# Fifteen transfers of a few bytes queued between the last pieces of an attention block's output weights

## The chip, the cores and the metric

The kernel runs on one core of a Trainium2 chip. It is one launch with bfloat16 inputs and a bfloat16 output. The metric is device microseconds (us) for one execution, and lower is better. A core has four compute engines that run side by side: TensorE (PE in the profile; its weight loads are listed as PEld), VectorE (DVE), ScalarE (ACT) and GpSimd (POOL). A fifth, SyncE (SP), issues data transfers. Sixteen DMA engines carry these transfers out. A transfer is issued by an engine's sequencer, waits in that issuer's queue, runs, and announces its end by counting up a semaphore.

## The reference: what is computed

One token `x` (1024 numbers) goes through two blocks, and a gate mixes their outputs. Cut to what matters:

```
q = x @ wq                            # 32 heads of 128
p = softmax(q . k_cache / sqrt(128))  # 4 key/value heads, 65536 positions, 8 query heads on each
a = (p . v_cache) @ wo                # wo: 4096 x 1024
z = gelu(x @ w_in);  z1, z2 = halves of z, z2 layer-normed
b = (z1 * (w_sp * z2 + b_sp)) @ w_out
g = sigmoid(sum(x * gate_w))
out = g * a + (1 - g) * b             # 1024 numbers
```

The caches are 64 MB each in bfloat16 and every byte of them is used once; `wo` and `wq` are 8 MB each. Reading them is most of what the kernel does: the trace counts 162.01 MB read.

## The kernel before, in words

**Memory.** One SBUF tensor, `arena`, holds everything. The list of regions after L190 gives each region its offset in order, so a region appended at the end moves none of the others. Its first region, `RING`, is five slots of 32 KB per partition that the large inputs pass through.

**The stream of loads.** `load` (L307) appends each large load to the list `stream`: `wq`, the keys, the two weights of the second block, then keys and values in turn, and last `wo`. `wo` is split in four quarters of 1024 rows. The first three are one transfer each. The last quarter is cut by `WO_CUT` into three pieces of 5/8, 2/8 and 1/8 (1280, 512 and 256 KB). I call them piece A, piece B and piece C. Each lies across all 128 partitions; a partition's share is one contiguous run of 10,240, 4,096 or 2,048 bytes.

**The order of the transfers.** `issue` (L376 to L391) walks the stream. It puts one `dma_start` (L389) on SP's queue for each entry, as soon as everything that used the target's place has been recorded as used, and stops at the first entry whose place is still needed. Instructions of one engine run in the order in which they are recorded, so SP issues the stream in its order, each entry after its wait. Just before the last entry, piece C, `issue` calls `store()` (L366) once: an early transfer of the still empty output row. The real store is recorded at the end of the program. Both are transfers of 8 rows of 256 bytes from `orow` to `out`.

**Waits.** The `Recorder` (L18) derives the waits. An operation that reads a key waits for the key's last writer; a DMA gets a semaphore of its own name (`dma=`), and a reader waits for that semaphore's full count of 16 (L108). Waits on other engines are at L110.

**The end of the program.** After the last values, `wo_rows` multiplies the first two quarters of `wo` with the attention output, `wo_piece(2)` the third quarter, and `wo_piece(3, c0, c1)` the three pieces of the last: 40, 16 and 8 matmuls at L712 into one accumulator `fbt`, each piece after its own load. `spin` runs a few matmuls whose result is not used. DVE then copies `fbt` to `orow` (L775), and SP stores it (L366). POOL has nothing to do after its copies at L490, the last of which ends near 245 us.

Of the kernel before, what the change touches and what calls it, by code (L numbers as in the profile page):

```python
# [138 lines left out]
def bass_gated_mix__gqa_block_cached__mixer_gmlp__decode_kernel(  # L139
# [23 lines left out]
    FC = FH // 128  # L163
# [12 lines left out]
    QW = DO // NW  # L176
# [11 lines left out]
    def region(name, nbf):  # L188
        nonlocal cur
        OFF[name] = cur  # L190
        cur += (nbf + 15) // 16 * 16

    for name, n in [
        ("RING", NSUB * SUB), ("KT", NKT * 4096), ("SC", NSC * 2048), ("PSB", 2 * 1024), ("PTSB", 2 * 1024),
        ("QPAD", 4 * QP), ("IDB", 128), ("BM", 256), ("SEL", 16 * 32),
        ("M16", 32), ("MQ", 32), ("XT", KC), ("WB", 2), ("WBB", 4), ("ONEB", 128),
        ("MAXC", 2 * total), ("LP", 2 * total), ("COLS", 2 * 64), ("DM", 64), ("ONES", 256), ("QALL", 128), ("OVZ", 32 * OC + 31), ("E4Z", 128), ("MHALF", 4),
        ("YB", FC), ("OROW", QW),
    ]:
        region(name, n)  # L200
    NA = (cur + 63) // 64 * 64
# [2 lines left out]
    def ab(name, n, o=0):  # L204
        return arena[:, OFF[name] + o:OFF[name] + o + n]
# [4 lines left out]
    def vw(base, off, dims, p0=0, np_=128):  # L210
        ps = base.ap[0][0]
        return bass.AP(tensor=base.tensor, offset=base.offset + off + p0 * ps,
                       ap=[[ps, np_]] + [list(d) for d in dims])
# [41 lines left out]
    P = R.op  # L255
# [46 lines left out]
    stream = []  # L302
# [42 lines left out]
    for i in range(6):  # L345
        a = 2 * i + 4
# [18 lines left out]
    def store():  # L365
        P("SP", lambda e: e.dma_start(out[0, 0].rearrange("(q n) -> q n", n=QW), osrc), r=["orow"],  # L366
          w=["out"], dma="out")

    issued = [0]
    used = set()  # L370
    owner = {}

    def grains(off, w):
        return list(range(off // GRAN, (off + w + GRAN - 1) // GRAN))

    def issue():  # L376

        while issued[0] < len(stream):
            n = issued[0]
            keys, off, src = stream[n]  # L380
            w = src.shape[1]
            gr = grains(off, w)
            if any(k not in used for x in gr if x in owner for k in owner[x]):
                return
            for j, x in enumerate(gr):
                owner[x] = (keys[j * len(keys) // len(gr)],)
            if n == len(stream) - 1:
                store()
            P("SP", lambda e, o=OFF["RING"] + off, w=w, src=src: e.dma_start(arena[:, o:o + w], src),  # L389
              w=[("slot", x) for x in gr], dma="s%d" % gr[0])  # L390
            issued[0] += 1  # L391

    def use(key):
        n, off, w = place[key]
        assert n < issued[0], key
        return arena[:, OFF["RING"] + off:OFF["RING"] + off + w], [("slot", x) for x in grains(off, w)]

    def done(key):
        used.add(key)
        issue()  # L400

    issue()


# [8 lines left out]
      r=["m32"], w=["sel"])  # L413
    P("DVE", lambda e: e.tensor_reduce(mq, vw(idf, 0, [[1, 16], [16, 8]]), AXX, ALU.add), r=["idf"], w=["mq"])
    P("DVE", lambda e: e.tensor_reduce(mhalf, vw(idf, 0, [[32, 2], [64, 2], [1, 32]]), mybir.AxisListType.XY, ALU.add),
      r=["idf"], w=["mhalf"])
# [4 lines left out]
    for fe in range(4):  # L421
        P("POOL", lambda e, fe=fe: e.tensor_copy(vw(sele, 128 * fe, [[32, 4], [1, 32]]),
                                                vw(idb, 64 * (fe // 2) + fe % 2, [[0, 4], [2, 32]])),
          r=["idb"], w=[KSE])
# [5 lines left out]
    def f(e):  # L430
        for c in range(KC):
            ins = e.matmul(tb[:, c:c + 1], vw(xm, c, [[8, 128]], 0, 8), oneb[0:8, 0:1], start=(c == 0),  # L432
                           stop=(c == KC - 1), skip_group_check=True)
        return ins
# [3 lines left out]
      r=["oneb", "wsp", "bsp"], w=["mb"])  # L438
# [6 lines left out]
      r=["ones", "gs"], w=[KTB])  # L445
# [4 lines left out]
      r=["g"], w=["omg"])  # L450
# [254 lines left out]
    def wo_piece(i, c0=0, c1=8):  # L705
        sl, keys = use(("wo", i, c0))
        def f(e, i=i, sl=sl, c0=c0, c1=c1):
            for c in range(c0, c1):
                for s, b, j in SLOTS:
                    o = DO * (c - c0) + QW * s  # L710
                    z = 31 + 32 * (8 * i + c) - j
                    ins = e.matmul(fb[32 * b:32 * (b + 1), 0:QW], ovz[:, z:z + 32],  # L712
                                   sl[:, o:o + QW], start=False, stop=(i == 3 and c == 7),
                                   tile_position=(0, 32 * b), skip_group_check=True)
            return ins
        P("PE", f, r=[("ovec", i)] + keys, w=["fb"])
        done(("wo", i, c0))
# [54 lines left out]
    spin(3)  # L772
    for c0, c1 in WO_CUT:
        wo_piece(3, c0, c1)
    P("DVE", lambda e: e.tensor_copy(orow[0:W0 + NW, :], fb[0:W0 + NW, 0:QW]), w=["orow", "fb"])  # L775
    store()

# [31 lines left out]
```

## Time and profile before

| | us |
|---|---|
| median of 3 runs | 381.85 (381.62 to 381.86) |
| span of the profiled execution, first to last instruction | 380.3 |
| what lies around the span (median less span) | 1.55 |
| PE busy | 235.1 |
| DVE busy | 204.6 |
| ACT busy, POOL busy | 23.3, 8.4 |
| DMA: mean rate over the span | 426 GB/s |

The profile is one execution of the program. Busy time says how long an engine worked; a wait is put down to what ended last before it. "Landing" is the moment at which a transfer's semaphore is full. Besides the views of the page, the trace keeps a record of each DMA packet (its queue, size, start and duration), and the moments at which each of the 16 parts of a transfer counted up its semaphore. A packet is one contiguous run of one partition, or the 4 bytes that close a transfer on one DMA engine. The records do not name the DMA engine.

### The profile page before, as it was taken

The numbers are of one execution on the slowest core, as the hardware profiler recorded it, in microseconds if no ns is written. First come the engines' busy times: TensorE is split into PE (matmuls) and PEld (weight loads), VectorE is DVE, ScalarE is ACT, GpSimd is POOL, SyncE is SP. The second block draws the span as 40 slices with busy tenths as digits, with TensorE's granted clock in tenths as the row PEclk, the third lists the DMA queues.
The fourth block names the chain that finished last, engine by engine and source line by source line (L and its number), as shares of the span: only waits on it lengthen the run. The fifth ranks groups of instructions, "written<-read, shape, count | busy, mean of one in ns | idle before, by whom it ended". The sixth has DMA issues, their size and how long they took to land.

```text
span 380.3 us, 2581 instructions
## 1 busy us (share of the span) xinstructions
PE 235.1 (62%) x1449; PEld 58.1 (15%) x836; DVE 204.6 (54%) x162; ACT 23.3 (6%) x24; POOL 8.4 (2%) x37
## 2 busy tenths in 40 slices
PE   0061388458558924895788138952895884739378
PEld 0010011011111200122112001220121110212015
DVE  4011496778389525965892249745774882312020
ACT  1000000010420000002200000022000000220000
POOL 5000000000000000000000000000000000000000
PEclk9998599696859985998699859995899697958689
DMA  9999999999999999999999999999999999999996
GB/s 435 427 420 400 469 388 438 441 469 431 401 414 441 441 443 427 434 410 424 477 441 434 434 434 414 415 441 441 434 407 433 445 441 441 436 403 424 419 426 262
DMA packets 4254, 162.17 MB, mean 426 GB/s; under 512 B 532, under 2 KB 532, under 8 KB 788
## 3 DMA queue, kind: packets, MB, share of 16 engines
q1 hardware_dynamic: 4208, 162.01, 98.9%
q8 instruction: 9, 0.15, 0.2%
q10 hardware_dynamic: 36, 0.00, 0.0%
q14 instruction: 1, 0.01, 0.0%
HBM read 162.01 MB, written 0.00 MB: 426 GB/s over the span
## 4 chain that ended last, share of the span: by engine, by line
DMA 56%; PE 23%; DVE 18%; ACT 1%; issue 1%; SPq 0%; ACTq 0%; DVEq 0%
DMA arena<-in_A_k_cache_dram 34%; DVE arena L502 15%; DMA arena<-in_A_wo_dram 10%; DMA arena<-in_A_v_cache_dram 8%; PE scp L260 7%; PE scp L262 6%; DMA arena<-in_B_b_sp_dram 5%; PE obt L260 4%; PE obt L262 4%; DVE arena L539 1%; PE fbt L712 1%; PE fbt L660 1%; ACT arena L534 1%; SPq L389 0%; ACTq L288 0%
## 5 line engine op out<-in xcount | busy, mean ns | idle before, releaser
L502 DVE STREAM_TRANSPOSE arena<-arena 128x2048 f32<-128x2048 f32 x64 | 143.0, 2284 | 48.2 <-DMA arena<-in_A_k_cache_dram 32.7
L260 PE MATMUL scp<-arena 128*128 128x512 bf16 (+1 forms) x275 | 112.8, 429 | 87.7 <-DVE arena L502 86.3
L262 PE MATMUL scp<-arena 128*128 128x512 bf16 (+1 forms) x279 | 113.1, 427 | 0.0
L260 PE MATMUL obt<-arena 128*64 128x512 bf16 (+2 forms) x334 | 62.9, 419 | 17.5 <-DMA arena<-in_A_v_cache_dram 17.5
L262 PE MATMUL obt<-arena 128*64 128x512 bf16 (+2 forms) x334 | 62.2, 414 | 0.0
L260 PEld LDWEIGHTS scp<-arena 128*128 128x128 bf16 (+1 forms) x275 | 27.7, 104 | 200.1 <-issue 101.3
L539 DVE STREAM_TRANSPOSE arena<-arena 128x2048 bf16<-128x2048 bf16 x7 | 16.2, 2311 | 28.5 <-PE obt L262 26.4
L534 ACT ACTIVATE arena<-arena 128x2048 bf16<-128x2048 f32 x8 | 16.0, 2002 | 218.6 <-DVE arena L531 195.6
L260 PEld LDWEIGHTS obt<-arena 128*64 128x64 bf16 (+1 forms) x334 | 18.3, 113 | 70.7 <-issue 56.1
L519 DVE TENSOR_SCALAR_CACHE_REDUCE arena<-scp 128x2048 f32<-128x2048 f32 x8 | 18.3, 2292 | 16.0 <-PE scp L262 16.0
L580 PE MATMUL mbt<-arena 128*128 128x128 bf16 x16 | 1.9, 258 | 12.6 <-DVE arena L575 12.6
L542 DVE STREAM_TRANSPOSE arena<-arena 128x1024 bf16<-128x1024 bf16 x2 | 2.5, 1246 | 12.7 <-PE obt L262 12.7
L490 POOL COPY arena<-arena 32x32 bf16<-32x32 bf16 x16 | 3.2, 203 | 234.5 <-PE scp L262 209.7
L568 DVE RECIPROCAL arena<-mbt 128x1 f32<-128x1 f32 x4 | 0.6, 139 | 14.1 <-PE mbt L563 14.1
L531 DVE TENSOR_REDUCE arena<-mbt 128x1 f32<-128x32 f32 x4 | 0.8, 192 | 13.5 <-PE mbt L528 13.5
L437 PE MATMUL mbt<-arena 1*128 1x2 bf16 x1 | 0.2, 158 | 12.3 <-DMA arena<-in_B_b_sp_dram 12.3
L439 DVE COPY arena<-mbt 128x2 f32<-128x2 f32 x1 | 0.2, 160 | 12.3 <-PE mbt L437 12.3
L775 DVE CAST arena<-fbt 36x128 bf16<-36x128 f32 x1 | 0.3, 283 | 11.0 <-PE fbt L712 11.0
L432 PE MATMUL scp<-arena 8*128 8x1 bf16 x8 | 0.7, 199 | 8.7 <-DVE arena L427 8.7
L712 PE MATMUL fbt<-arena 128*32 128x128 bf16 x128 | 4.1, 220 | 0.1
L712 PEld LDWEIGHTS fbt<-arena 128*32 128x32 bf16 x128 | 3.6, 97 | 1.6 <-DMA arena<-in_A_wo_dram 0.8
L467 DVE CAST arena<-obt 97x1024 bf16<-97x1024 f32 x1 | 1.2, 1225 | 4.9 <-PE obt L262 4.9
(91 smaller groups left out, 54.2 us busy)
## 6 DMA issues: line engine op xcount, KB each, us to landing
arena<-in_A_k_cache_dram SPq DMA_DIRECT2D x6, 4096.0 KB, 33.1
arena<-in_A_v_cache_dram SPq DMA_DIRECT2D x2, 4096.0 KB, 26.0
arena<-in_B_w_in_dram SPq DMA_DIRECT2D x1, 7168.0 KB, 30.4
arena<-in_A_wo_dram SPq DMA_DIRECT2D x3, 2048.0 KB, 33.4
arena<-in_B_w_out_dram SPq DMA_DIRECT2D x1, 3584.0 KB, 21.5
arena<-in_A_wo_dram SPq DMA_DIRECT2D x1, 1280.0 KB, 30.3
arena<-in_A_wo_dram SPq DMA_DIRECT2D x1, 512.0 KB, 31.0
arena<-in_A_wo_dram SPq DMA_DIRECT2D x1, 256.0 KB, 30.8
```

The source lines that it names most:

```text
L260: return e.matmul(*a, **kw)
L262: one = e.matmul(*a, **kw).ins
L467: P("DVE", lambda e: e.tensor_copy(psb[0:97, :], ob[0:97, :]), w=["psb", "ob"])
L490: P("POOL", lambda e, pb=pb: e.tensor_copy(vw(qpad, 24 + 32 * pb, [[QP, 4], [1, 8]], 32 * pb, 32), vw(qall, 8 * g, [[32, 4], [1, 8]], 32 * ...
L502: P("DVE", lambda e: e.transpose(ktb(i).bitcast(F32), sl[:, 4096 * p:4096 * (p + 1)].bitcast(F32)), r=keys[4 * p:4 * p + 4], w=[("kt", i % ...
L519: P("DVE", lambda e: e.tensor_scalar(scs(j), scp[:, :], 0.0, None, op0=ALU.add, op1=ALU.max, accum_out=maxc[:, j:j + 1]), w=[("sc", j % 2) ...
L534: P("ACT", lambda e: e.activation(psb2, scs(j), ACTF.Exp, bias=gcol(j // 2, K_NB), scale=SCALE, accum_out=lp[:, j:j + 1]), r=[("sc", j % 2 ...
L539: P("DVE", lambda e: e.transpose(ptsb2, psb2), r=["psb"], w=[("ptsb", 0), ("ptsb", 1)])
L542: P("DVE", lambda e: e.transpose(ptsb(n), ab("PSB", 1024, 1024 * (n % 2))), r=["psb"], w=[("ptsb", n % 2)])
L580: ins = e.matmul(mb[:, 0:128], sel[:, 128 * c:128 * (c + 1)], osc[:, 128 * c:128 * (c + 1)], start=(c == 0), stop=(c == 3))
L660: ins = e.matmul(fb[32 * b:32 * (b + 1), 0:QW], e4z[0:97, 31 - j:63 - j], part[0:97, QW * s:QW * (s + 1)], start=(first and s % (NW // 2) ...
L712: ins = e.matmul(fb[32 * b:32 * (b + 1), 0:QW], ovz[:, z:z + 32], sl[:, o:o + QW], start=False, stop=(i == 3 and c == 7), tile_position=(0 ...
```

## The change

A strip `PRB` of 32 elements (64 bytes) per partition is added at the end of the list of regions. A function `prefixes` queues fifteen transfers on SP. The transfer number k reads two bfloat16 numbers (4 bytes) from each of the first k rows of `A_wq` and puts them into the first k partitions of the strip, at a place of their own. They are issued after piece A of the last quarter of `wo` and before piece B. Each has a semaphore of its own. One POOL copy of one element, recorded after the last matmuls, waits for all fifteen. Nothing reads that element.

```diff
-        ("YB", FC), ("OROW", QW),
+        ("YB", FC), ("OROW", QW), ("PRB", 32),
...
+    prb = ab("PRB", 32)
+
+    def prefixes():
+        for k in range(1, 16):
+            def f(e, k=k):
+                with nc.allow_non_contiguous_dma(reason="a few bytes"):
+                    return e.dma_start(prb[0:k, 2 * k:2 * k + 2], A_wq[0:k, 2 * k:2 * k + 2])
+            P("SP", f, w=[("prb", k)], dma="p%d" % k)
...
             P("SP", lambda e, o=OFF["RING"] + off, w=w, src=src: e.dma_start(arena[:, o:o + w], src),
               w=[("slot", x) for x in gr], dma="s%d" % gr[0])
             issued[0] += 1
+            if n == len(stream) - 3:
+                prefixes()
...
     for c0, c1 in WO_CUT:
         wo_piece(3, c0, c1)
+    P("POOL", lambda e: e.tensor_copy(prb[0:1, 0:1], prb[0:1, 2:3]), r=[("prb", k) for k in range(1, 16)], w=["prb0"])
     P("DVE", lambda e: e.tensor_copy(orow[0:W0 + NW, :], fb[0:W0 + NW, 0:QW]), w=["orow", "fb"])
     store()
```

## The prediction, as it was put on record before the change was run

> **What bounds the kernel.** I read the page first: the busy shares, then the DMA rows, then the chain of waits at the very end, then SP's own timeline. PE is busy 62% of the span and DVE 54%, but the DMA engines are full from the first slice to the last but one:
>
> ```profile
> DMA  9999999999999999999999999999999999999996
> ...
> q1 hardware_dynamic: 4208, 162.01, 98.9%
> q8 instruction: 9, 0.15, 0.2%
> q10 hardware_dynamic: 36, 0.00, 0.0%
> ```
>
> The row of digits is the share of the 16 DMA engines in use; q1 is SP's queue and fills 98.9% of them. So the transfers of SP are the bound, and whatever is put into them ahead of the last one is on the path, unless the DMA engine that carries it has time to spare. The chain of waits, cut to its last microseconds, shows who waits for that last one:
>
> ```profile
> 376.41 0.08 issue
> 376.50 1.77 PE fbt L712 x56
> 378.27 0.01 issue
> 378.27 0.42 PE fbt L712 x8
> ...
> 378.79 0.28 DVE arena L775
> ```
>
> and the timeline of the same stretch, with the idle time and its releaser in brackets:
>
> ```profile
> 378.27 0.23 PEld L712 LDWEIGHTS fbt<-arena 128*32 128x32 bf16 x8 [0.18 <-DMA arena<-in_A_wo_dram]
> 378.79 0.28 DVE L775 CAST arena<-fbt 36x128 bf16<-36x128 f32 x1 [11.04 <-PE fbt L712]
> 379.10 0.31 SPq L366 DMA_DIRECT2D out_dram<-arena  x1
> ```
>
> The 56 matmuls of pieces A and B are issued by 378.27, and the 8 of piece C start there. PE's weight loads had been idle for 0.18 us, waiting for piece C. A delay of piece C is therefore passed on in full to PE, DVE and the store. An earlier piece C could gain at most about that 0.18 us.
>
> **How far SP is ahead of the DMA engines.** SP's timeline (start, duration), then the DMA issues of the page (KB, us to landing):
>
> ```profile
> 345.71 1.28 SPq L389 DMA_DIRECT2D arena<-in_A_wo_dram  x3
> 347.03 0.37 SPq L366 DMA_DIRECT2D out_dram<-arena  x1
> 347.44 0.35 SPq L389 DMA_DIRECT2D arena<-in_A_wo_dram  x1
> ```
>
> ```profile
> arena<-in_A_wo_dram SPq DMA_DIRECT2D x1, 1280.0 KB, 30.3
> arena<-in_A_wo_dram SPq DMA_DIRECT2D x1, 512.0 KB, 31.0
> arena<-in_A_wo_dram SPq DMA_DIRECT2D x1, 256.0 KB, 30.8
> ```
>
> The three issues from 345.71 are the third quarter, A and B: 1.28 / 3 = 0.43 us each. C follows at 347.44. A starts about 346.1 and lands 30.3 later, at 376.4; B at 346.55 + 31.0 = 377.6; C at 347.44 + 30.8 = 378.2. The DMA engines reach B some 28 us after it was issued, because that much work lies in the queue before it.
>
> **The change, part by part.**
>
> *Fifteen issues on SP.* They stand before B, the early store and C. The nearest rows are the issues of few rows:
>
> ```profile
> L288 ACTq DMA_DIRECT2D arena<-in_A_x_dram x1: 562/562/562, 0.1 to 0.1; - x1
> L288 ACTq DMA_DIRECT2D arena<-in_B_w_sp_dram x1: 273/273/273, 1.0 to 1.0; - x1
> L366 SPq DMA_DIRECT2D out_dram<-arena x2: 309/338/367, 347.0 to 379.1; - x2
> ```
>
> With 0.04 us between issues, fifteen take between 15 x 0.31 = 4.7 and 15 x 0.60 = 9.0 us; I take 15 x 0.41 = 6.2, by the early store's 0.37 + 0.04. C is then issued at 353.6 (at most 356.4) in place of 347.44. The first DMA engine finishes A at about 375, so 18 us of cover are left. SP's next work, the real store, waits for DVE until 379.10. Cost: nothing. Without the cover it would be the whole 6.2 us.
>
> *Packets in the DMA queues.* The page's q10 row tells how a small transfer is cut. ACT issues two transfers of 8 rows and two of one element, and q10 has 36 packets: 2 x (8 + 8) + 2 x (1 + 1). So a transfer of k rows uses k DMA engines, with one data packet and one closing packet on each. The fifteen add 1 + 2 + ... + 15 = 120 data and 120 closing packets. If the first k engines are taken each time, the first engine gets 15 pairs, the eighth 8, the ninth 7, the fifteenth 1, the sixteenth none. "DMA: Bandwidth & Descriptors" of the Trainium skill, section "Why a DMA increments its semaphore by 16 and not by 1", states just this choice of the lowest-numbered k; the trace does not name engines.
>
> What does a pair cost? In the packet records one engine's packets follow each other end to start. On q10 a 2-byte packet starts at 13.849 and the engine's next one at 13.854; closing packets of 4 bytes hold their engine 6 ns as well, and a 256-byte row of the early store 14 ns. A pair is about 12 ns, 28 at the most if a 4-byte row is as dear as a 256-byte row and its closing packet too.
>
> Now which engine is last. C's 16 closing counts come at 376.57 to 376.65 (five), 376.96, 377.06, and 377.89 to 378.23 (nine). Of the nine late chains of packets, three carry a row of the early store, so they belong to the first eight engines; their closing packets start at 377.43, 377.50 and 377.54. The other six have none, so they are among the second eight; theirs start from 377.58 to 377.815, and the last of these ends the load (378.23).
> - A late engine of the first eight has 0.27 us to spare against 377.815. Fifteen pairs of 12 ns are 0.18 us: hidden. At 28 ns they are 0.42: 0.15 late.
> - A late engine of the second eight has at most 7 pairs: 7 x 12 = 0.08 us, or 0.20 at 28 ns; at least none. These come straight on top.
> - The five early engines have 1.6 us to spare.
>
> So C lands 0 to 0.08 us later by the likely price, 0.20 by the dear one. I take 0.05.
>
> A rule of the skill speaks against the change: the same page's "Anatomy of one DMA" gives a fixed cost of about 2.0 us for a DMA (on another issue path than SP's), and its "Rules for kernel authors" call transfers under 64 KB mostly overhead. Paid one after another that would be an estimate of 15 x 2.0 = 30 us. The trace has a 2 KB store queued between B and C, and C still lands 0.63 us after B, about its own 8 rows a DMA engine; so here the fixed part overlaps.
>
> *The POOL copy.* It is queued behind nothing; POOL's last work is the copies at L490 (200 ns each, ending near 245 us), and nothing is behind it. Its waits end when A's engines have passed A and the pairs, near 376.8. A semaphore wait of POOL lasts 17 ns in the trace; with fifteen and one copy of 0.2 us, POOL is done by about 378, before the end at 380.3. It reads the strip and holds up nobody; if the waits took 0.2 us each it would end at 380 and still not be last. Cost: nothing.
>
> *The strip.* It is appended, so no other region moves. Cost: nothing.
>
> **Sum.** The profiled execution spans 380.3 us; 0 + 0.05 + 0 + 0 makes 380.35. The median is 1.55 us above that span, for what lies around it; I add the same: 381.9.
>
> **The rivals.**
> 1. *A run of tiny packets stalls its DMA engine* (slower). The trace never shows more than three packets of at most 256 bytes in a row on one engine (B's closing packet, the store's row and its closing packet), and 30 in a row may drain what the engine fetches ahead. The bound is one slot of the smallest large row, 2,048 bytes, 80 ns start to start, for each packet, 160 for a pair. A late engine among the second eight then pays up to 7 x 0.16 = 1.1 us; one of the first eight up to 15 x 0.16 - 0.27 = 2.1. From 0.3 to 2.1, I take 1.1: 383.0. It decides as soon as a pair on the last engines costs over 0.1 us. For it: nothing but the missing row. Against it: the 6 ns that every single small packet takes.
> 2. *A limit on transfers in flight on SP's queue* (slower). In the trace at most nine are in flight (from 347.44 until the next value landing at 348.9); with the change B would be about the 22nd. With a limit near 16, the last issues wait for landings and B waits for A, at 376.4. The real store needs 0.78 us from its issue (379.10) to its first packet (379.88), so B starts about 377.2, takes 1.25, C then 0.64 and 0.41 to land: 379.5 against 378.2, or +1.3: 383.15. Against it: four issues in a row at 0.43 us with six to nine in flight.
> 3. *A closing packet holds the engine until the data before it has landed* (slower). The lag from a closing packet's start to its count is 0.41 us. Seven pairs would be 2.9 us on the second eight, fifteen 6.2 on the first: 384.7 to 388. Against it: C's rows start 6 ns after the early store's closing packet.
> 4. *One more instruction fetch* (slower). q8 has nine packets of 16 KB, about 1.0 us each on one engine. If the new instructions call for a tenth, on a late engine before C: 0.6 (its data at the usual rate) to 1.0, so 382.6. Against it: PE has nearly all of the instructions, and none is added there.
> 5. *Faster.* I find no mechanism over the 0.18 us of PE's wait. *That the change does nothing at all* is the forecast's lower end, 381.85.
>
> **How the numbers follow.** The forecast has 0.60, rival 1 0.14, rival 2 0.12, rival 3 0.05, rival 4 0.05, and an unseen gain 0.04. The forecast's own range is 381.65 to 382.3: the lowest run before, and the dear pair plus the spread of the runs. Rivals 1, 2 and 4 reach 383.2 for most of their mass; rival 3, the upper part of rival 1 and the gain are left out, about 0.15 in all. So the range is 381.6 to 383.2. Within 0.2% means within 0.76 us, about what a measurement of this kernel can tell from no change; the forecast and the cheap end of rivals 1 and 4 lie in it: 0.64. Slower by more: 0.32. Faster: 0.04.
>
> **What would show it.** Right: SP's fifteen issues of 0.3 to 0.6 us each before B, B and C issued 5 to 9 us later, their time to landing shorter by the same, PE's 8 last matmuls at 378.3 to 378.5, q1 with 240 packets more, POOL's copy before the end. Wrong by rival 1 or 3: C's counts late on the DMA engines with most pairs, with gaps after the tiny packets. By rival 2: SP's issues stretched, each ending with a landing. By rival 4: ten packets on q8. The prediction fails outright if the last engines of C turn out to be among those with many pairs and a pair costs over 0.1 us.

## The result and the profile after

| | before | after |
|---|---|---|
| median, 5 runs of each | 381.85 us (381.62 to 381.89) | 383.18 us (382.94 to 383.33) |
| ratio after / before | | 1.0034, 95% interval 1.0023 to 1.0045 |
| span of the profiled execution | 380.3 us | 381.6 us |

The change makes the kernel 1.33 us slower. That is beyond the 0.2% that I called no change, and just inside the range on record. The line numbers after the diff are up to 12 higher: the large loads are at L398, the fifteen at L375, the matmuls of the last quarter at L723.

The page of the changed kernel has nearly the same DMA row (an 8 in two slices that had a 9), and q1 has 240 packets more (4,208 before), as counted from the fifteen:

```profile
DMA  9999989999999999999999999999989999999996
...
q1 hardware_dynamic: 4448, 162.01, 98.8%
q8 instruction: 9, 0.15, 0.2%
q10 hardware_dynamic: 36, 0.00, 0.0%
```

The end of the chain of waits (start, duration, what) is where the time went:

```profile
351.10 0.38 SPq L375
351.48 0.04 issue
351.52 27.36 DMA arena<-in_A_wo_dram
378.88 0.04 issue
378.93 0.62 PE fbt L723 x16
379.58 0.42 PE fbt L723 x8
380.05 0.04 issue
380.09 0.28 DVE arena L787
```

Before, PE issued pieces A and B without a gap from 376.50, and only the 8 matmuls of piece C waited, until 378.27. Now the 16 matmuls of B wait until 378.93 and C's until 379.58. The timeline shows the same wait at PE, and POOL's copy, which ended its wait before the end of the program:

```profile
376.49 1.29 PE L723 MATMUL fbt<-arena 128*32 128x128 bf16 x40 [0.44 <-DMA arena<-in_A_wo_dram]
378.49 0.18 POOL L786 COPY arena<-arena 1x1 bf16<-1x1 bf16 x1 [133.58 <-DMA arena<-in_A_wq_dram]
378.93 1.05 PE L723 MATMUL fbt<-arena 128*32 128x128 bf16 x24 [1.14 <-DMA arena<-in_A_wo_dram]
380.09 0.28 DVE L787 CAST arena<-fbt 36x128 bf16<-36x128 f32 x1 [10.99 <-PE fbt L723]
```

PE, DVE and the store behind C are as long as before. A lands at 376.35 (376.36 before), B at 378.88 (377.60), C at 379.53 (378.23). So 1.3 us came in between A and B: where the fifteen stand.

SP was not what made B late. Its timeline:

```profile
346.20 5.27 SPq L375 DMA_DIRECT2D arena<-in_A_wq_dram  x15
351.52 2.37 SPq L398 DMA_DIRECT2D arena<-in_A_wo_dram  x1
353.93 4.83 SPq L366 DMA_DIRECT2D out_dram<-arena  x1
358.81 0.56 SPq L398 DMA_DIRECT2D arena<-in_A_wo_dram  x1
```

The fifteen take 5.27 us. Then three issues stretch (2.37 us, 4.83 us and 0.56 us in place of 0.43, 0.37 and 0.35), but C is still issued at 358.81, 16 us before the first DMA engine is done with A.

**The moments at which the parts of a transfer count up its semaphore** tell the rest. The last counts of the transfers with 6 to 15 rows, then of B and C:

```
rows  6       7       8       9       10      11      12      13      14      15      B       C
      376.44  376.66  376.88  377.12  377.33  377.54  377.75  377.95  378.14  378.35  378.88  379.53
```

Each count of a transfer appears in the next one about 0.2 us later; the transfer with 6 rows adds one count that those of 5 rows had not, 376.44. So it is the engine that joins with the sixth row, which I call the sixth, that comes last. It ended A at 376.2, and then ended one tiny transfer in every 0.21 us: ten pairs of a data packet and a closing packet, 2.1 us. Other engines show the same pace: the first three, which ended A about 374.75, end their pairs between 377.2 and 377.5. In the packet records the pairs start 6 ns apart, as the prediction had it; it is their ends that are 0.2 us apart. Behind the pairs, B takes 0.53 us on the sixth engine, where it took 1.24 before. So 2.1 us of pairs cost 2.1 - 0.7 = 1.4 there. I call these 0.7 us "made good"; that the engine reads on while the ends wait is how I explain them.

The packet records show the wait one step later, in the packets that an engine takes up behind the pairs. Before, each of B's 128 packets took 0.16 to 0.17 us. Now 20 of them take over 0.2 us, the longest 1.49, and together they are 11 us longer on the 16 engines.

### The profile page after: what moved, and what is told of

It reads as the page before. It is cut to its first block, busy times and chain, and to the rows that moved or that the text cites. A ratio compares the mean times of both kernels' runs of the same rounds, so it can differ in the third digit from the quotient of the medians.

```text
span 381.6 us, 2604 instructions
## 1 busy us (share of the span) xinstructions
PE 233.6 (61%) x1449; PEld 58.0 (15%) x836; DVE 204.5 (54%) x162; ACT 23.2 (6%) x24; POOL 9.6 (3%) x38
## 4 chain that ended last, share of the span: by engine, by line
DMA 63%; DVE 17%; PE 17%; SPq 2%; issue 1%; ACTq 0%; DVEq 0%
DMA arena<-in_A_k_cache_dram 41%; DVE arena L513 15%; DMA arena<-in_A_v_cache_dram 9%; DMA arena<-in_A_wo_dram 7%; DMA arena<-in_B_b_sp_dram 5%; PE scp L260 5%; PE scp L262 4%; PE obt L260 3%; PE obt L262 3%; SPq L375 1%; DVE arena L550 1%; ACTq L288 0%; SPq L398 0%; PE fbt L723 0%; DVE arena L584 0%
## 5 line engine op out<-in xcount | busy, mean ns | idle before, releaser
L260 PE MATMUL scp<-arena 128*128 128x512 bf16 (+1 forms) x275 | 110.9, 420 | 86.1 <-DVE arena L513 86.0
L262 PE MATMUL scp<-arena 128*128 128x512 bf16 (+1 forms) x279 | 110.3, 414 | 0.0
L260 PE MATMUL obt<-arena 128*64 128x512 bf16 (+2 forms) x334 | 64.0, 424 | 19.2 <-DMA arena<-in_A_v_cache_dram 19.2
L262 PE MATMUL obt<-arena 128*64 128x512 bf16 (+2 forms) x334 | 63.4, 420 | 0.0
L723 PE MATMUL fbt<-arena 128*32 128x128 bf16 x128 | 4.3, 220 | 2.5 <-DMA arena<-in_A_wo_dram 2.5
L723 PEld LDWEIGHTS fbt<-arena 128*32 128x32 bf16 x128 | 3.6, 97 | 4.3 <-DMA arena<-in_A_wo_dram 3.1
```

The lines of the kernel that those rows point to most:

```text
L260: return e.matmul(*a, **kw)
L262: one = e.matmul(*a, **kw).ins
```

## The experiments

Times are medians beside runs of the kernel before on the same chip (381.82 to 381.87). Each edit is against the changed kernel, except where it says otherwise; POOL's copy waits for as many transfers as there are, and its edit isn't shown.

**Is it the data packets or the closing packets?** Three theories: the closing packet has to wait for its own data (R), writing 4 bytes is slow (N), or a run of packets drains what is fetched ahead (P, rival 1 of the prediction).

```diff
-        for k in range(1, 16):
...
-                    return e.dma_start(prb[0:k, 2 * k:2 * k + 2], A_wq[0:k, 2 * k:2 * k + 2])
+                return e.dma_start(vw(prb, 0, [[4, 15], [1, 2]], 0, 16),
+                                   A_wq[0:16, 0:60].rearrange("p (j c) -> p j c", c=4)[:, :, 0:2])
```

> One transfer of 16 rows replaces the fifteen: each row has 15 separate runs of 4 bytes, so each of the 16 DMA engines gets 15 tiny data packets but one closing packet. Theory R (a closing packet has to wait until its own data are written, about 0.2 us for a tiny transfer, and holds what follows): one such wait, 381.85 to 382.05. Theory N (writing 4 bytes costs the 0.2 us, the closing packet nothing): 15 x 0.2 = 3.0 us on every engine, less the 0.7 that the changed kernel's slowest engine made good, 384.1. Theory P (a run of small packets drains what the engine has fetched ahead, so each packet costs about 0.1 us): 16 x 0.1 - 0.7 = 0.9, 382.75.

Measured: 382.08 (1.0007, interval 0.9998 to 1.0016), 0.03 above what R had at most. The page has the 240 data and 16 closing packets more:

```profile
q1 hardware_dynamic: 4464, 162.01, 98.9%
```

Sixteen small packets in a row on every engine, the last one to land included, cost nothing that this measurement can tell. The one closing packet counts 0.18 to 0.25 us after A's on each engine. N and P fall: they had 384.1 and 382.75. The run takes away fourteen closing packets and, with them, fourteen transfers; whether it is the closing packet or something else that comes once for each transfer on an engine, this and the runs below don't tell apart.

**Is it the size of the data?** Fifteen transfers again, rows of 512 bytes in an unused part of the key buffers:

```diff
-                    return e.dma_start(prb[0:k, 2 * k:2 * k + 2], A_wq[0:k, 2 * k:2 * k + 2])
+                    o = 512 + 256 * (k - 1) if k < 15 else 6144
+                    return e.dma_start(ab("KT", 256, o)[0:k, :], A_wq[0:k, 256 * k - 256:256 * k])
```

> The fifteen transfers as in the change, with rows of 512 bytes in place of 4, written into a part of a key buffer that is no longer used. Theory R: as the change, 383.2, and up to 0.2 more for the larger data. Theory N: only the time of the data remains, 10 x 0.02 = 0.2 us on the engine that decided, which is below its head start; 381.85 to 382.1. Theory P: as the change, 383.2.

Measured: 383.06 (1.0032, 1.0021 to 1.0044), as the change. Rows 128 times as long cost the same; N falls a second time.

**Do neighbouring writes wait for each other?** The 4 bytes of each transfer are put 256 bytes apart:

```diff
-                    return e.dma_start(prb[0:k, 2 * k:2 * k + 2], A_wq[0:k, 2 * k:2 * k + 2])
+                    return e.dma_start(ab("KT", 2, 512 + 128 * (k - 1))[0:k, :], A_wq[0:k, 2 * k:2 * k + 2])
```

> The change with the 4-byte writes 256 bytes apart in each partition, in place of 4 bytes apart inside 64 bytes. Theories R, N and P: no difference from the change, 383.2. Theory L (successive writes into the same short stretch of a partition have to wait for each other): the cost goes, 381.9.

Measured: 383.05 (1.0031, 1.0019 to 1.0043), as the change. L falls.

**Does the last engine set the price?** Only the transfers of 1 to 5 rows are left:

```diff
-        for k in range(1, 16):
+        for k in range(1, 6):
```

> Only the first five transfers (1 to 5 rows). They use the first five DMA engines alone, of which four land piece A 1.4 us or more before the last engine and the fourth 0.6 us before. If the time is set by the engine that lands last and a pair costs 0.2 us there (theories R, N, L), five pairs at most are hidden: 381.85, within 0.15. If the cost is one of the queue or of SP's issues as a whole, a third of 1.33 us is left: 382.3.

Measured: 381.83 (1.0000, 0.9992 to 1.0009). Five transfers cost nothing, and a third of the price for a third of the transfers (382.3) falls. That these engines were early is one reason; the other is that five are hardly more than the four that cost nothing even on every engine (run with four, below), so this run alone doesn't show that the last engine sets the price. The counts of the changed kernel do: its first three engines have 13 to 15 pairs and end them between 377.2 and 377.5, and the sixth, with ten, at 378.35. The end of this run's chain has the shape of the kernel before, with the last matmuls issued without a gap:

```profile
345.25 31.23 DMA arena<-in_A_wo_dram
376.48 0.14 issue
376.61 2.15 PE fbt L723 x64
378.77 0.03 issue
```

**Does the place in the queue matter?** The fifteen stand before the first quarter of `wo` (`len(stream) - 7`), or behind piece C (`len(stream) - 1`):

```diff
-            if n == len(stream) - 3:
+            if n == len(stream) - 7:
```

> The fifteen transfers of the change stand before the first quarter of the output weights in place of before piece B, some 8 MB earlier in the queue. Theory R (each closing packet waits about 0.2 us for its own data and holds what follows on its engine, and the large transfers behind run at full pace already, so that the lost time isn't made good): as the change, 383.1. Rival: the 0.7 us that were made good in the 1.9 us of pieces B and C show that the engine can catch up, so 18 us of large transfers make good all of it: 381.9.

Measured: 382.85 (1.0024, 1.0014 to 1.0035). The transfer with 15 rows lands at 360.50, the second quarter of `wo` at 369.53 (368.38 before) and C at 379.39 (378.23): the delay is 1.15 us in both places, and stays so through the large transfers between them. Some 0.7 us are made good at once here too: the first quarter of `wo` lands 4.13 us after the fifteenth, where before it landed 4.89 after the value transfer ahead. Nothing more is made good behind it; that rival falls.

> The fifteen transfers stand behind piece C, the last one. Theory R: piece C lands as in the kernel before; only the real store, 8 rows on the first eight engines, is behind them. On the sixth engine 10 pairs end 2.0 us after its part of piece C, at about 380.2, so the store ends 0.2 to 0.4 later: 382.1. If the fifteen cost something as instructions or semaphores, wherever they stand: 383.2.

Measured: 382.54 (1.0019, 1.0010 to 1.0028). C lands at 378.25, as in the kernel before. My number, 382.1, missed: the store does end only 0.12 us later (380.42), but POOL's copy, which waits for the fifteen, is now the last to end. The chain inside the span hangs on it:

```profile
362.92 17.30 DMA arena<-in_A_wq_dram
380.23 0.02 issue
380.25 0.04 POOLq L108
380.29 0.08 issue
380.37 0.18 POOL arena L786
```

But most of the 0.67 us by which the median is longer lies outside the span: the median span of the eleven executions is 380.6, that of the kernel before beside them 380.55, while what lies around the span is 1.68 to 1.95 us in each of the eleven and 1.26 to 1.43 before. Why it grows when POOL ends last no run here shows.

**Is it the number of rows below 16?** All fifteen with 16 rows:

```diff
-                    return e.dma_start(prb[0:k, 2 * k:2 * k + 2], A_wq[0:k, 2 * k:2 * k + 2])
+                    return e.dma_start(prb[0:16, 2 * k:2 * k + 2], A_wq[0:16, 2 * k:2 * k + 2])
```

> All fifteen transfers have 16 rows, so every one of the 16 engines gets 15 pairs. Theory R: the engine that lands last pays 15 x 0.2 = 3.0 us, less about 0.7 made good: 384.15. Rival S (the cost comes with transfers that use fewer than 16 engines, whose missing counts somebody else has to add): gone, 381.9.

Measured: 384.44 (1.0064, 1.0052 to 1.0077). S falls, R had 384.15. The chain now waits longer for B and C:

```profile
379.73 0.04 issue
379.77 0.62 PE fbt L723 x16
380.39 0.04 issue
380.43 0.42 PE fbt L723 x8
```

A ends at 376.58, the fifteenth tiny transfer at 379.20: 2.62 us, 0.175 for each. B follows after 0.53 us and C after another 0.66, as in the change.

**Does it hold with another queue?** The fifteen on ACT's queue:

```diff
-            P("SP", f, w=[("prb", k)], dma="p%d" % k)
+            P("ACT", f, w=[("prb", k)], dma="p%d" % k)
```

> The fifteen transfers are issued on ACT's queue in place of SP's, at the same place in the program. The profile before shows packets of the two queues taking turns on an engine, so each pair stands beside a packet of 16 or 32 KB of SP's queue. Theory R with a wait that holds only the queue of the closing packet: hidden, 381.9. Theory R with a wait that holds the whole engine: as the change, 383.2.

Measured: 381.94 (1.0004, 0.9995 to 1.0012): hidden. ACT issues them as soon as it gets there, some 11 us before SP did:

```profile
335.13 2.18 ACTq L375 DMA_DIRECT2D arena<-in_A_wq_dram  x7
337.34 3.07 ACTq L375 DMA_DIRECT2D arena<-in_A_wq_dram  x8
```

They land one by one between 341 and 365, the last counts of successive transfers 0.6 to 2.5 us apart, with SP's large packets in between. So the pairs are the same 240 packets on the same engines, and cost nothing when each has a large packet after it. Whether it is the other queue or the distance that helps, this run doesn't tell: the two came together.

**How does the price grow?** Four and eight transfers of 16 rows:

```diff
-        for k in range(1, 16):
+        for k in range(1, 5):
...
-                    return e.dma_start(prb[0:k, 2 * k:2 * k + 2], A_wq[0:k, 2 * k:2 * k + 2])
+                    return e.dma_start(prb[0:16, 2 * k:2 * k + 2], A_wq[0:16, 2 * k:2 * k + 2])
```

> Four transfers of 16 rows of 4 bytes: 4 x 0.175 = 0.70 us on every engine. If an engine makes good about 0.7 us behind a run of them, as the change and the fifteen full ones showed, nothing is left: 381.85 to 382.05. If the cost is in proportion to their number (2.57 us for fifteen): 382.55.

Measured: 381.93 (1.0003, 0.9994 to 1.0011). Four cost nothing that can be told, though every engine carries them.

> Eight transfers of 16 rows of 4 bytes: 8 x 0.175 - 0.7 = 0.7, 382.55. In proportion to the fifteen: 8 x 2.57 / 15 = 1.37, 383.2.

Measured: 382.68 (1.0022, 1.0013 to 1.0030). Four, eight and fifteen cost 0.1, 0.9 and 2.6 us: nothing that can be told for the first four, then 0.19 each up to eight and 0.24 each up to fifteen. So it isn't a price in proportion. The line n x 0.2 - 0.7 gives 0.1, 0.9 and 2.3; it is 0.3 short at fifteen, whose profiled execution, from which the 0.175 come, was the fastest of its five (383.87).

B's packets agree. With four, none of the 128 takes over 0.19 us; with eight, 32 take over 0.2 us, the longest 0.81; with fifteen 48, the longest 1.71. Added up and shared among 16 engines, they are 0.02, 0.6 and 2.1 us longer than 0.159 us each.

**Does every transfer pay it?** The kernel before, the third quarter of `wo` cut into eight:

```diff
-    for i in range(3):
+    for i in range(2):
         load([("wo", i, 0)], rows(A_wo, i, 8), WO_AT[i])
+    for c in range(8):
+        load([("wo", 2, c)], rows(A_wo, 2, 8)[:, DO * c:DO * (c + 1)], WO_AT[2] + DO * c)
...
-    wo_piece(2)
+    for c in range(8):
+        wo_piece(2, c, c + 1)
```

> The kernel before, without the fifteen; the third quarter of the output weights comes as eight transfers of 256 KB in place of one of 2 MB, each with its own matmuls. Seven closing packets are added on every engine, 0.64 us of data apart. Theory R with a short wait that the engine makes good while large data follow: 381.9. Rival (every closing packet costs its 0.18 us, wherever it stands): 7 x 0.18 = 1.26, 383.1, or 382.4 if 0.7 of it is made good at the end.

Measured: 382.31 (1.0015, 1.0006 to 1.0024). R's 381.9 and the rival's 383.1 missed; the rival's 382.4, with 0.7 made good at the end, lies within the interval, so the time doesn't decide. The counts do: by the rival the eight would land about 0.64 + 0.18 = 0.82 us apart. They land 0.68 us apart where a strip of this size takes 0.64 + 0.01 by its packets and 0.61 in one large transfer. Shorter rows move a little more slowly (2,048 bytes in 80 ns, 16,384 in 607 ns), which is 0.03 us of each piece, or about 0.3 in all, and 0.03 are left for the closing packet. It doesn't pay 0.18 us where 0.64 us of data follow. The profiled execution is the longest of the eleven (383.71), and for a reason of its own: PE's granted clock in the last 4 us is 0.57, and the last 64 matmuls take 3.52 us (2.18 before). PE had waited 1.9 us for A; that the wait lowered the clock isn't shown, as in the next run PE waited 1.7 us for A and the clock stayed at 1.00 (columns: stretch, length, busy time of PE, PEld, DVE, ACT, POOL with their instructions, PE clock, DMA share, GB/s):

```profile
374.00:377.00 3.00, 1.16 (x24) 0.49 (x16) 0.00 (x0) 0.00 (x0) 0.00 (x0) 1.00 0.91 372
377.00:381.00 4.00, 3.52 (x64) 3.28 (x64) 0.15 (x1) 0.00 (x0) 0.00 (x0) 0.57 0.17 66
```

**Does the wait come on top of the data, or beside them?** Eight transfers of 16 rows of 2,048 bytes, into the score buffer:

```diff
-        for k in range(1, 16):
+        for k in range(1, 9):
...
-                    return e.dma_start(prb[0:k, 2 * k:2 * k + 2], A_wq[0:k, 2 * k:2 * k + 2])
-            P("SP", f, w=[("prb", k)], dma="p%d" % k)
+                    return e.dma_start(ab("SC", 1024, 1024 * (k - 1))[0:16, :], A_wq[0:16, 1024 * ((k - 1) % 4):1024 * ((k - 1) % 4) + 1024])
+            P("SP", f, w=[("prb", k)] + ([("sc", 0), ("sc", 1)] if k == 1 else []), dma="p%d" % k)
```

> Eight transfers of 16 rows at the place of the fifteen, each row 2,048 bytes (0.08 us of an engine), written into the score buffer that is no longer used; its output is the reference's. Theory R1 (a closing packet waits about 0.18 us after its own data, and the next data wait behind it): 0.26 us for each pair, 8 x 0.26 - 0.7 = 1.4, 383.25. Theory R2 (an engine only ends one transfer in 0.18 us; the data of the next one are written meanwhile): 0.18 us for each pair, 8 x 0.18 - 0.7 = 0.74, 382.6, which is also what the data alone need at the usual rate.

Measured: 385.20 (1.0086, 1.0073 to 1.0100), far above both. The experiment has an effect of its own. Its DMA engines are busy, but move little (columns as above):

```profile
374.00:376.00 2.00, 1.88 (x64) 1.80 (x65) 0.00 (x0) 0.00 (x0) 0.00 (x0) 1.00 1.08 271
376.00:378.00 2.00, 0.60 (x2) 0.00 (x0) 0.00 (x0) 0.00 (x0) 0.00 (x0) 1.00 1.05 199
378.00:380.00 2.00, 1.29 (x40) 1.15 (x40) 0.00 (x0) 0.00 (x0) 0.00 (x0) 1.00 0.84 158
```

Busy for the whole of the time, they move 199 to 271 GB/s, after 418 in the two microseconds before. Even A's and B's packets take longer there (4,096 bytes 0.29 us in the middle in place of 0.16). All 256 KB go into the first 16 partitions, and the engines seem to meet there. "DMA: Bandwidth & Descriptors" of the Trainium skill, section "The descriptor swizzle", puts these 16 partitions on the ports that four engines use in a transfer over 128 partitions; by that, an estimate from 32,768 bytes in 1.213 us on one engine is 262,144 bytes / (4 x 27 GB/s) = 2.4 us. No other run here tests it. So the question between R1 and R2 stays open.

## Why the prediction was right and wrong

**What bounds the kernel: right.** The DMA engines are full, and the delay of C went straight to PE, DVE and the store.

**SP's issues at no cost: right, with a miss beside it.** 5.27 us for the fifteen (6.2 taken). I had not foreseen that three issues after them stretch by 6.6 us; C was issued at 358.81, later than the 356.4 that I gave as the latest. The cover of 18 us became 16 and was enough.

**What a pair costs: wrong, and this is the step that failed.** I took 12 ns, 28 at the most. It is 0.175 to 0.21 us. I read the price from when an engine *starts* its next packet, and from single small packets. The starts are indeed 6 ns apart in the changed kernel too, so the gaps after the tiny packets that I named as the sign of rivals 1 and 3 aren't there; but the counts of short transfers follow each other at 0.2 us, and B's packets behind them are held up instead. The trace of before had the other number: the lag of 0.41 us from a closing packet's start to its count, which I used for rival 3 only.

**Which engine is last: the method was right, the engine another one.** I gave the last place to an engine of the second eight with at most 7 pairs and 0.27 us of head start to late ones of the first eight. With 0.2 us for a pair, a late engine with more pairs wins: the sixth, with ten. The head start was too small to hide them.

**The rivals.** Rival 1 had nearly the time (383.0) but not the cause: sixteen small packets in a row cost nothing in the one-transfer run. Rival 3, a closing packet that holds its engine until its data have landed, comes nearest to what the runs show, a cost for each transfer and not for its packets or bytes, at too high a price (0.41 us for a pair, nothing made good; at least 384.7); that it is the closing packet that waits isn't shown. What I set against it, that C's rows start 6 ns after the store's closing packet, was no evidence, as the starts run ahead of the ends. Rival 2 is half there: SP's issues do stretch, as I said they would in that case, but only one of the three ends near a landing, and B waited for nothing from them. Rival 4: q8 still has nine packets.

**POOL and the strip: right.** POOL is done at 378.67 (about 378 forecast), 2.9 us before the end. With the fifteen last in the queue it was POOL that ended last: the copy's cost was nothing only as long as what it waits for came early.

**The numbers.** The range (381.6 to 383.2) held 383.18 by luck: its upper end came from rivals 1, 2 and 4, none of which happened. The likeliest case, and with it the 0.64 for no change, was wrong, and the last sentence of the prediction describes what came: a last engine with many pairs, and a pair that costs over 0.1 us. The 1.55 us around the span set a median against the span of one execution; the executions of the kernel before have 1.26 to 1.46 each. As it was taken off and put back, the 381.9 doesn't depend on it. The missing row, several small transfers in a row on one engine, was named as missing, but the value was taken from the single ones.

What I weighed of "DMA: Bandwidth & Descriptors" of the Trainium skill, a fixed cost of about 2.0 us for each DMA ("Anatomy of one DMA", for another issue path) and small transfers as mostly overhead ("Rules for kernel authors"), pointed the right way; the 0.2 us here are about a tenth of it. A sentence of the same page that I had not weighed, in "Queues, rings and completion order", says that the count of a semaphore lands only after every earlier write of that DMA engine. The run with one closing packet agrees with it. That this shows the cause in the chip is an inference: what exactly waits for 0.2 us no run here shows.

## What to carry to other kernels

In this kernel, where the DMA engines are the bound, small transfers in a row in one queue cost about 0.2 us each on every engine that they use, with 4 bytes a row as with 512, less about 0.7 us for the whole run of them; so put what is small into one transfer with many runs, or give it a queue on which it stands alone between large packets. What counts is the engine that lands the last piece: look at the 16 counts of that piece first, and then at how many small transfers lie before it on that engine. A packet's start says when an engine took it up, not when it was free of it: price a transfer by the distance of the counts, and look at how long the packets behind it take.

## What the runs showed of the hardware that was not expected

- A run of short transfers ends one per 0.175 to 0.21 us on each engine, while their packets start 6 ns apart; the wait shows in the packets behind them (4,096 bytes in up to 1.49 us in place of 0.16). With large data behind each, the wait can't be seen (0.68 us for a piece of 0.65).
- An engine made good about 0.7 us behind such a run (B in 0.53 us in place of 1.24), once; a delay of 1.15 us then stayed through 4 MB of large transfers.
- SP's issues stretched with many small packets queued: 2.37 and 4.83 us, the latter ending at 358.76, 0.16 us after a value transfer ahead had landed (358.60). In the run with one transfer of 256 packets C's issue took 3.68 us.
- Sixteen engines that write 256 KB into 16 partitions move 199 GB/s, and packets to other partitions in the same queue are slowed with them.
